# Attention into an expert layer on one Trainium2 core: weight conversion cut into single operations, scores and values on two shared banks, and a changed order of the fold

## The chip, the cores and the metric

The kernel runs on one core of a Trainium2 chip. The metric is the device time of one execution in microseconds (us). A core has TensorE (PE, with its weight loads as PEld), VectorE (DVE), ScalarE (ACT), GpSimd (POOL) and SyncE (SP), which here issues every transfer; TensorE writes to eight banks of PSUM memory, and VectorE and ScalarE empty them.

## The reference

Eight batches of 12 heads, 448 positions, 64 columns a head. The heads' scores are mixed with each other ahead of the softmax and behind it; the attention output is the input of an expert layer without a nonlinearity.

```python
scores = scale * np.matmul(q, k.transpose(0, 1, 3, 2))
scores = np.einsum('bhij,hg->bgij', scores, w_pre)
attn = np.exp(scores - np.max(scores, axis=-1, keepdims=True))
attn = attn / (np.sum(attn, axis=-1, keepdims=True) + 1e-09)
attn = np.einsum('bhij,hg->bgij', attn, w_post)
x = np.matmul(attn, v)                     # then (B*S, H*D) = (3584, 768)
a = x @ w1                                 # 768 x 1024
b = x @ w2
h = a * b @ w3                             # 1024 x 1024
out = h @ w_out                            # 1024 x 768
```

The expert weights come as 64-bit floats, and the kernel turns them into 32-bit floats itself.

## The kernel before

**The loop.** `run` walks through 360 steps, 45 a batch. A step handles 10 query rows of all 12 heads as one tile of 120 rows. In step n `softmax(n)` takes the row minimum (`mn`, VectorE L246, of negated scores) and the exponential (`e`, ScalarE L249); `scale(n-1)` makes the weights of the second mixing (`sa`, `ri`, `w`, VectorE); `split_r(n+2)` splits fetched scores into a high and a low part (`rh` on VectorE L226, `rl` on GpSimd L227); `post(n-2)` mixes the exponentials (`pso`, TensorE L272, bank 4), and ScalarE copies the result into `mt` (L278) at the end of the step; `mix(n+1)` mixes the next scores (`psm`, banks 2 and 3). Each engine runs its instructions strictly in the order in which the program issues them, and that order is written out here by hand: by this loop, by tables of steps, and by the lists `ends`, `soon` and `later`, which hold copies, second parts and stores back to the end of the step or to the next one.

**Scores.** Those of batch 0 (`qk_first`, `psz`, L158) come in 24 units, the last 18 of them in steps 0 to 14. Those of later batches come from `qk` (`psq`, L193 and L194, two matmuls a unit, 48 units a batch), ahead of `post` in their step, on banks 0 and 1 in turn; ScalarE copies them into `st` (L198), and they go to memory (`raw_d`) and come back as `r` four steps ahead of their use. `split_kq` makes the operands of a head: ScalarE writes `qh` (L181, 128 partitions, from queries that were loaded twice, `load_kq`) and half of `kk` (L182), GpSimd the low parts `ql` (L183) and the other half of `kk` (L184). Batch 1's units lie in steps 12 to 37, those of a later batch b in 45 steps from 45(b-1) - 6.

**Values.** In steps 17, 20, 32, 35, 47, 50 and so on (six a batch) `av` multiplies finished columns of `mt` with the values (`psa`, L303), in bank 5 up to the pair stage. Behind it ScalarE copies the result out (`xh` or `xd`), and in batch 0 VectorE takes the low part (`xl`).

**Conversion.** A piece of weights (128 x 384) is loaded as words (`cs`), ScalarE squares its upper words (`cm`, L102), VectorE makes four operations on it (`ca`, `ca`, `ca`, `cx`, L112 to L116, with bank 5 between them), ScalarE and GpSimd split the result into two parts (`two_parts`, L121 and L122: `fo`, `fw` or `wu`). A generator (`converting`) does a whole piece in a step, and none in a step with values, since those hold bank 5. 40 pieces belong to the fold, 32 to the two first weights.

**Fold and experts.** `folding` multiplies w3 with w_out into one matrix (`psf`, L361, 16 groups of 24 matmuls in banks 6, 7 and 1), in the background of steps 2 to 48; `share` says how many matmuls a step takes, and `there(p)` how many the pieces p made so far allow. From step 50 (`SWITCH`) the background are experts: batch 0 and 1 alone (`eg`, `eo`, L523 and L554, from step 53, `E_AT`, on) and, from step 187 (`PAIR`), three pairs of batches (`e`, L703) to the end. The first weights are converted from step 48 on while batch 0's experts use them (up to `LATE`, step 107).

## Time and profile before

| | us |
|---|---|
| median of 3 runs | 1639.13 (1638.95 to 1643.07) |
| the profiled execution | 1639.43 |
| its span in the profile | 1637.7 |
| TensorE busy | 1579.9 (96%) |
| VectorE busy | 1030.6 (63%) |
| ScalarE busy | 997.3 (61%) |
| GpSimd busy | 1068.5 (65%) |
| transfers | 446.10 MB, 272 GB/s on average |

Spans and busy times are those of the one profiled execution. A row of the profile names a line, an engine, an operation and its tiles as out<-in; the figures are busy time, the mean of one, and the idle time of the engine just ahead, with what ended it. Matmuls are pipelined, and their ends are modelled, so TensorE may be busy in the profile and still be below its pace: the distance of one step's `psm` to the next tells more.

### The profile page before, as it was taken

The page shows a single profiled execution, that of the slowest core. Times are in us where ns is not written, and L with a number is a line of the kernel's source. Part 1 is how long each engine was busy: PE and PEld are TensorE (multiplying, and loading weights), DVE is VectorE, ACT ScalarE, POOL GpSimd, SP SyncE. Part 2 cuts the span into 40 slices and gives each one's busy share as a digit, 9 for nine tenths or more (in the row PEclk, how much of TensorE's full clock was granted, in tenths as well). Part 3 has the DMA queues.
Part 4 walks back from the last instruction along what each step waited for, and adds up shares of the span by engine and source line. Part 5 has one row for each costly group of instructions (what it writes and reads, how often), then busy time and mean ns, then how long its engine had stood idle before and what let it go on. Part 6 is the DMA issues. An engine that isn't in the chain of part 4 may idle for free. (4 is left out here: it accounts for less than half of the span.)

```text
span 1637.7 us, 31687 instructions
## 1 busy us (share of the span) xinstructions
PE 1579.9 (96%) x10528; PEld 1414.0 (86%) x10528; DVE 1030.6 (63%) x2302; ACT 997.3 (61%) x2413; POOL 1068.5 (65%) x902
## 2 busy tenths in 40 slices
PE   5999999999999999999999999999999999999999
PEld 2578997887898888889899898899999898999988
DVE  5967768778747767863465565745555557634573
ACT  4877657677666776776666666666765554542321
POOL 1346546667657788885576776876675666655774
PEclk7999999999999999999999999999999999999999
DMA  8988879898899999999978977889978756678875
GB/s 263 342 269 275 255 223 302 277 310 288 264 279 310 321 341 315 323 335 306 312 240 279 290 243 238 257 270 309 305 248 250 238 188 196 211 229 302 281 233 179
DMA packets 233906, 446.10 MB, mean 272 GB/s; under 512 B 21838, under 2 KB 159054, under 8 KB 233678
## 3 DMA queue, kind: packets, MB, share of 16 engines
q1 hardware_dynamic: 233742, 444.08, 84.6%
q8 instruction: 83, 1.36, 0.4%
q14 instruction: 81, 0.66, 0.1%
HBM read 309.90 MB, written 134.09 MB: 271 GB/s over the span
## 5 line engine op out<-in xcount | busy, mean ns | idle before, releaser
L227 POOL TENSOR_TENSOR rl<-r,rh 120x448 fp32r<-120x448 f32 (+1 forms) x340 | 425.0, 1250 | 321.9 <-DVE rh L226 108.0
L246 DVE TENSOR_REDUCE mn<-psm 120x1 f32<-120x448 f32 x360 | 223.8, 622 | 410.1 <-PE psm L240 395.1
L249 ACT ACTIVATE e<-psm,mn 120x448 f32<-120x448 f32 x360 | 228.5, 635 | 348.1 <-DVE sa L258 293.4
L272 PEld LDWEIGHTS pso<-w,e 120*112 120x112 f32 (+1 forms) x2880 | 345.5, 177 | 49.4 <-ACT mt L278 35.0
L272 PE MATMUL pso<-w,e 120*112 120x120 f32 (+1 forms) x2880 | 358.9, 267 | 20.6 <-ACT mt L278 20.2
L703 PE MATMUL e<-eh,wu 128*128 128x448 f32 x1008 | 304.4, 371 | 1.1 <-DVE c L657 1.1
L278 ACT COPY mt<-pso 112x480 f32<-112x480 f32 x360 | 206.9, 575 | 14.9 <-PE pso L272 9.9
L703 PEld LDWEIGHTS e<-eh,wu 128*128 128x128 f32 x1008 | 187.3, 188 | 16.1 <-DVE c L657 1.9
L226 DVE CAST rh<-r 120x448 fp32r<-120x448 f32 (+1 forms) x340 | 189.9, 559 | 4.1 <-DMA r<-raw_d 3.0
L703 PE MATMUL e<-el,wu 128*128 128x448 f32 x504 | 187.6, 372 | 2.4 <-POOL el L642 2.4
L198 ACT COPY st<-psq 112x448 f32<-112x448 f32 x336 | 173.3, 527 | 25.8 <-DMA raw_d<-st 25.7
L303 PE MATMUL psa<-mt,v 112*64 112x150 f32 (+1 forms) x2304 | 156.9, 292 | 1.9 <-DMA v<-v 1.9
L183 POOL TENSOR_TENSOR ql<-kq,qh 128x448 fp32r<-128x448 f32 x84 | 99.2, 1181 | 85.1 <-ACT qh L181 84.9
L303 PEld LDWEIGHTS psa<-mt,v 112*64 112x64 f32 x2304 | 143.6, 137 | 8.1 <-DMA v<-v 2.3
L657 DVE TENSOR_TENSOR c<-c,e 128x448 f32<-128x448 f32 x168 | 101.2, 615 | 70.4 <-PE e L703 65.8
L193 PE MATMUL psq<-kk,qh 128*112 128x448 f32 x336 | 125.7, 374 | 8.0 <-ACT st L198 7.8
L238 PE MATMUL psm<-rh,wph 120*120 120x448 f32 (+1 forms) x340 | 129.6, 381 | 0.0
L523 PE MATMUL eg<-xh,wu 128*128 128x448 f32 x384 | 127.3, 381 | 0.0
L240 PE MATMUL psm<-rl,wph 120*120 120x448 f32 (+1 forms) x340 | 124.1, 365 | 0.6 <-POOL rl L227 0.5
L239 PE MATMUL psm<-rh,wpl 120*120 120x448 f32 (+1 forms) x340 | 124.2, 365 | 0.0
L194 PE MATMUL psq<-kk,ql 128*112 128x448 f32 x336 | 122.8, 365 | 0.0
L642 POOL TENSOR_TENSOR el<-x,eh 128x448 fp32r<-128x448 f32 x90 | 105.7, 1195 | 9.3 <-DMA x<-x_d 5.3
(114 smaller groups left out, 2961.7 us busy)
## 6 DMA issues: line engine op xcount, KB each, us to landing
r<-raw_d SPq DMA_DIRECT2D x352, 210.0 KB, 4.1
raw_d<-st SPq DMA_DIRECT2D x168, 392.0 KB, 4.7
wu<-w_d SPq DMA_DIRECT2D x104, 384.0 KB, 5.6
wu<-s_d SPq DMA_DIRECT2D x96, 384.0 KB, 4.4
v<-v SPq DMA_DIRECT2D x144, 224.0 KB, 5.1
kq<-kq SPq DMA_DIRECT2D x42, 672.0 KB, 7.0
wu<-w_d SPq DMA_DIRECT2D x51, 512.0 KB, 5.9
wu<-s_d SPq DMA_DIRECT2D x36, 512.0 KB, 4.4
```

The source lines that it names most:

```text
L193: nc.tensor.matmul(p, qh[:, cols], kk, start=True, stop=False)
L198: copy(st[:, c % 2], p)
L226: nc.vector.tensor_copy(rh[:K], r[:K])
L227: nc.gpsimd.tensor_tensor(rl[:K], r[:K], rh[:K].bitcast(F32), op=ALU.subtract)
L238: nc.tensor.matmul(p[:K, :S], self.wph[:K, :K], rh[:K], start=True, stop=False)
L246: nc.vector.tensor_reduce(mn[:K], p[:K, :S], axis=AX.X, op=ALU.min)
L249: nc.scalar.activation(e[:K], p[:K, :S], AF.Exp, bias=mn[:K], scale=-1.0, accum_out=sm[:K])
L272: nc.tensor.matmul(p[:, j, :, :w], e[:K, j * JT:(j + 1) * JT], w2[:K, :, :w], start=True, stop=True)
L278: self.ends.append((4, lambda: copy(dst, p[:, :, :, :w])))
L303: nc.tensor.matmul(self.psa[rows, g % 3, :W], v[:, j, rows], mt[:, j, 2 * g + s, :W], start=(j == 0), stop=(j == NJ - 1))
L523: nc.tensor.matmul(p, u[:, k % (K1 // 2), x], xs[y][:, k], start=(k == 0 and t == 0), stop=(k == K1 - 1 and t == 2))
L703: nc.tensor.matmul(p, w[:, k, x], ops[m, k][y], start=(k == 0 and t == 0), stop=(k == nk - 1 and t == 2))
```

## The change

- Conversion goes by single operations. `begin_conversion`, ahead of the softmax, splits the piece made before and squares the next; `convert` issues one VectorE operation. Up to step 48 a step makes four, none in step 0; afterwards two in even and three in odd steps, steps with values included, as far as `room` lets it run ahead of the matmuls.
- Values take one of the banks 0 and 1, in turn with the scores (`turn`), until the pair stage. Bank 5 is the conversion's alone.
- Batch 1's scores lie in steps 16 to 40, those of batch b in 45 steps from 45(b-1) - 4, none in a step with values. A step's first unit stays ahead of `post`; a second and third come behind it.
- The fold takes w3's columns and w_out's halves in another order: pieces come as w3's columns 0, w_out's first half, w3's columns 1, w_out's second half, then the other columns; the first four groups are (0, 0), (1, 0), (0, 1), (1, 1), so the second needs no more of w_out than the first. The even spread begins at step 16 (`FOLD`); ahead of it 24 matmuls may be done up to step 9 and 48 up to step 15, as far as the pieces made allow. `SWITCH` is 49, `E_AT` is 51.
- Queries are loaded once per pair of heads (2 instead of 3 planes, three buffers instead of two). ScalarE copies them into both halves of `qh`; `ql` has two fixed tiles, zeroed at the start in the half that isn't written.
- At the start the remaining queries of pair 0 are loaded ahead of `wpre`; step 0 has one unit of first scores instead of two.

Two places in the order. The first is TensorE in steps 11 and 12 (`psz` first scores, `psq` batch 1's scores, `psf` fold, `pso` second mixing). Before:

```order
L235 MATMUL psm11_742<-r11_549,wsc_138 120x448
L158 MATMUL psz2_3_0_769<-kqz2_126 112x448
L158 MATMUL psz2_3_1_770<-kqz2_126 112x448
L272 MATMUL pso9_782<-w29_712,e9_650 112x120 x4
L235 MATMUL psm12_787<-r12_593,wsc_138 120x448
L158 MATMUL psz3_3_0_817<-kqz3_127 112x448
L158 MATMUL psz3_3_1_818<-kqz3_127 112x448
L193 MATMUL psq1_0_0_824<-kk1_0_694,qh1_0_692 112x448
L194 MATMUL psq1_0_0_824<-kk1_0_694,ql1_0_693 112x448
L193 MATMUL psq1_0_1_829<-kk1_0_694,qh1_0_692 112x448
L194 MATMUL psq1_0_1_829<-kk1_0_694,ql1_0_693 112x448
L272 MATMUL pso10_839<-w210_765,e10_707 112x120 x4
```

In the changed kernel, the same engine and steps:

```order
L238 MATMUL psm11_724<-r11_536,wsc_143 120x448
L160 MATMUL psz2_3_0_750<-kqz2_130 112x448
L160 MATMUL psz2_3_1_751<-kqz2_130 112x448
L365 MATMUL psf0_1_765<-fo_147,fw1_677 128x384 x4
L275 MATMUL pso9_770<-w29_689,e9_635 112x120 x4
L365 MATMUL psf0_1_765<-fo_147,fw1_677 128x384 x5
L238 MATMUL psm12_780<-r12_580,wsc_143 120x448
L160 MATMUL psz3_3_0_802<-kqz3_131 112x448
L160 MATMUL psz3_3_1_803<-kqz3_131 112x448
L365 MATMUL psf0_1_765<-fo_147,fw1_677 128x384 x4
L275 MATMUL pso10_821<-w210_745,e10_684 112x120 x4
L365 MATMUL psf0_1_765<-fo_147,fw1_677 128x384 x5
```

Nine fold matmuls of the second group (w3's second columns, w_out's first half) stand in each of these steps, and the scores of batch 1 have left step 12.

The second place is step 90, where weights are converted for the experts. VectorE before (`rh` splits scores, `ca` and `cx` are the conversion):

```order
L246 TENSOR_REDUCE mn90_5312<-psm90_5304 120x1
L258 TENSOR_SCALAR sa89_5317<-sm89_5262 96x1
L259 RECIPROCAL ri89_5318<-sa89_5317 96x1
L262 TENSOR_SCALAR w289_5319<-wpo_140,ri89_5318 96x12x8
L226 CAST rh92_5323<-r92_5194 120x448
L112 TENSOR_SCALAR ca66_5338<-cs66_5226 128x384
L113 SCALAR_TENSOR_TENSOR ca66_5338<-cs66_5226,ca66_5338 128x384
L114 SCALAR_TENSOR_TENSOR ca66_5338<-cs66_5226,ca66_5338 128x384
L116 SCALAR_TENSOR_TENSOR cx66_5342<-cm66_5336,ca66_5338 128x384
L246 TENSOR_REDUCE mn91_5367<-psm91_5356 120x1
```

VectorE after the change:

```order
L249 TENSOR_REDUCE mn90_5311<-psm90_5294 120x1
L261 TENSOR_SCALAR sa89_5316<-sm89_5259 96x1
L262 RECIPROCAL ri89_5317<-sa89_5316 96x1
L265 TENSOR_SCALAR w289_5318<-wpo_145,ri89_5317 96x12x8
L229 CAST rh92_5322<-r92_5202 120x448
L138 SCALAR_TENSOR_TENSOR cx65_5330<-cm65_5254,ca65_5278 128x384
L131 TENSOR_SCALAR ca66_5334<-cs66_5181,ca66_5334 128x384
L249 TENSOR_REDUCE mn91_5364<-psm91_5351 120x1
```

Two conversion operations stand ahead of the next minimum instead of four. ScalarE in the same step before (`st` a score copy, `ea` an expert copy):

```order
L249 ACTIVATE e90_5314,sm90_5315<-psm90_5304,mn90_5312 120x448
L198 COPY st3_1_2_5277<-psq3_1_3_5327 112x448
L121 CAST wu25_5333<-cx65_5290 128x3x128
L102 ACTIVATE cm66_5336<-cs66_5226 128x384
L529 COPY ea0_5_5360<-eg0_5_0_5176 128x448
L278 COPY mt1_2_4644<-pso88_5348 112x48x10
L249 ACTIVATE e91_5369,sm91_5370<-psm91_5356,mn91_5367 120x448
```

ScalarE after:

```order
L252 ACTIVATE e90_5313,sm90_5314<-psm90_5294,mn90_5311 120x448
L201 COPY st3_1_0_5274<-psq3_1_1_5326 112x448
L201 COPY st3_1_2_5346<-psq3_1_2_5343 112x448
L281 COPY mt1_2_4640<-pso88_5338 112x48x10
L146 CAST wu25_5359<-cx65_5330 128x3x128
L116 ACTIVATE cm66_5362<-cs66_5181 128x384
L252 ACTIVATE e91_5366,sm91_5367<-psm91_5351,mn91_5364 120x448
```

The split `wu` and the square `cm` moved from ahead of `mt` to between `mt` and the next exponential.

The diff, cut to its core:

```diff
-    def converting(self, jobs):
...
-            if 0 <= n < len(jobs):
-                made = self.to_f32(s, m, f"{self.n_made}")
-                self.n_made += 1
-            yield
+    def ask_words(self):
+        if self.c_asked < len(self.c_jobs):
+            self.c_words.append(self.words(self.c_jobs[self.c_asked][0], f"{self.c_asked}"))
+            self.c_asked += 1
+
+    def begin_conversion(self):
+        if self.c_made is not None:
+            self.c_jobs[self.c_parts][1](self.c_made)
+            self.c_made = None
+            self.c_parts += 1
+        if self.c_square is None and self.c_words:
+            s = self.c_words[0]
+            m = self.cx.tile([128, CW], F32, tag="m", name=f"cm{self.c_piece}", bufs=1)[:, :s.shape[1]]
+            self.nc.scalar.activation(m, s[:, :, 1].bitcast(F32), AF.Square)
+            self.c_square = m
+
+    def convert(self):
...
+        if self.c_op == 0:
+            self.ask_words()
+            self.c_a = self.bank(5, f"ca{self.c_piece}").bitcast(I32)[:, :n]
+        a = self.c_a
+        if self.c_op == 0:
+            nc.vector.tensor_scalar(a, top, 3, 0x3FFFFFFF, op0=ALU.logical_shift_left, op1=ALU.bitwise_and)
+        elif self.c_op == 1:
...
+        else:
...
+            self.c_made, self.c_square = x, None
+            self.c_words.pop(0)
+            self.c_piece += 1
+        self.c_op = (self.c_op + 1) % 4
     def load_kq(self, b, p):
-        t = self.kp.tile([128, 3, S], F32, tag="kq", name=f"kq{b}_{p}")
+        t = self.kp.tile([128, 2, S], F32, tag="kq", name=f"kq{b}_{p}", bufs=3)
...
-        ql = self.kp.tile([128, S], F32R, tag="ql", name=f"ql{b}_{h}")
+        ql = self.low_q[s]
...
-        nc.scalar.copy(qh, t[:, s])
-        nc.scalar.copy(kk[a], t[a, 2])
-        q_lo.tensor_tensor(ql, t[:, s], qh.bitcast(F32), op=ALU.subtract)
-        k_lo.tensor_tensor(kk[z], t[a, 2], kk[a].bitcast(F32), op=ALU.subtract)
+        nc.scalar.copy(qh[a], t[a, 0])
+        nc.scalar.copy(kk[a], t[a, 1])
+        nc.scalar.copy(qh[z], t[a, 0])
+        q_lo.tensor_tensor(ql[a], t[a, 0], qh[a].bitcast(F32), op=ALU.subtract)
+        k_lo.tensor_tensor(kk[z], t[a, 1], kk[a].bitcast(F32), op=ALU.subtract)
...
-            self.i_psa = self.next_bank() if self.pairs else 5
+            self.i_psa = self.next_bank() if self.pairs else self.turn()
...
-        yield from columns[0]
         for q in range(2):
+            yield from columns[q]
             for k in range(KF):
...
-        for f in range(1, KF):
+        for f in range(2, KF):
             yield from columns[f]
...
+        order = [(0, 0), (1, 0), (0, 1), (1, 1)] + [(f, half) for f in range(2, KF) for half in range(2)]
+        for n, (f, half) in enumerate(order):
+            w = self.fw[f]
+            i = 6 + n % 2 if n else 1
...
+    def turn(self):
+        self.n_turn += 1
+        return self.n_turn % 2
...
+        self.low_q = [cp.tile([128, S], F32R, name=f"ql{s}") for s in range(2)]
+        for s in range(2):
+            nc.gpsimd.memset(self.low_q[s][(1 - s) * D:(2 - s) * D].bitcast(F32), 0.0)
...
+        nc.sync.dma_start(self.kq0s[0][:, JT + S:], self.kq0[0][:, JT + S:])
         w = self.kp.tile([128, S], F32R, tag="qh", name="wpre_s").bitcast(F32)[:GI, :GI]
...
-            firsts.setdefault((u - HP) * 15 // (HP * NJ - HP), []).append((u % HP, u // HP))
+            firsts.setdefault((u - HP - 1) * 14 // (HP * NJ - HP - 1) + 1, []).append((u % HP, u // HP))
...
-            first, per, ahead = (12, 26 / 48, 2) if b == 1 else ((b - 1) * NB - 6, 45 / 48, 3)
+            first, last, ahead = (16, 41, 2) if b == 1 else ((b - 1) * NB - 4, b * NB - 4, 3)
+            steps = [n for n in range(first, last) if n not in avs]
             for u in range(H * NJ):
                 h, c = divmod(u, NJ)
-                n = first + int(u * per)
+                n = steps[u * len(steps) // (H * NJ)]
...
+                    n = max(n - ahead, lasts[-2] + 1)
+                    splits.setdefault(n, []).append((b, h))
...
-        FOLD, SWITCH, E_AT = 18, NB + 5, NB + 8
+        FOLD, SWITCH, E_AT = 16, NB + 4, NB + 6
...
+            if n < 4:
+                self.softmax(n)
+            p = self.c_parts
+            if p < len(self.c_jobs):
+                self.begin_conversion()
+            if 4 <= n < N:
                 self.softmax(n)
...
+            qk(qks.get(n, [])[:1])
+            for _ in range(4 if 0 < n < SWITCH else n and 2 + n % 2):
+                i = self.c_piece
+                if not self.c_words or self.c_op == 3 and not self.c_square:
+                    break
+                if self.c_op == 0:
+                    if i < n_fold:
+                        f = (i - 2 * KF) // 3
+                        room = f < 2 or done >= (KF * 3 * 3 if f == 2 else 2 * KF * 3 * (f - 1))
                     else:
...
+                        room = i == n_fold and n == SWITCH - 1 or n >= SWITCH and 2 * done >= 3 * K1 * (i - n_fold - 4)
+                    if not room:
+                        break
+                self.convert()
...
             if n < SWITCH:
-                wanted += now
-                now = max(min(there(p), KF * 3 + wanted) - done, 0)
+                now = min(spread(n, SWITCH - 1, total), 18) if n >= FOLD else 0
+                now = min(there(p), max(done + now, KF * 3 * (1 if n < 10 else 2 if n < FOLD else 3))) - done
+            elif n < LATE:
+                now = min(3 * K1 // 2 * (p - n_fold) - done, spread(n, LATE, E_1))
...
             for x in avs.get(n, []):
                 self.av(*x)
+            qk(qks.get(n, [])[1:])
```

More of the change, by code (lines that the diff above doesn't have):

```diff
@@ L872, in run @@
             self.fetch(n)
-        next(fold_pieces)
-        next(fold_pieces)
+        piece()
         held()
-        next(fold_pieces)
-        next(fold_pieces)
+        piece()
         self.split_r(0)
@@ L911, in run @@
             if n == PAIR:
-                assert done >= 2 * E_1 + E_2 and unit_pieces is None and not self.jobs and not self.ys
+                assert done >= 2 * E_1 + E_2 and self.c_parts == len(self.c_jobs) and not self.jobs and not self.ys
                 self.do_ends()
```

178 lines of the change are left out of this document (71 added, 107 removed).

## The prediction

> **What bounds the kernel now.** I read the busy time by stretches first, with the cuts laid at step boundaries: steps 0 to 2 of the loop end at 38.7 us, step 9 at 64, step 19 at 112, step 47 at 243, step 56 at 276.4, step 104 at 451.7. Columns: length, then busy time (and instructions) of TensorE, its weight loads, VectorE, ScalarE and GpSimd, the granted clock, the share of the transfer engines, GB/s.
>
> ```profile
> 0.00:38.70 38.70, 21.89 (x58) 8.49 (x59) 19.30 (x42) 15.38 (x33) 4.92 (x9) 0.78 0.86 256
> 38.70:64.00 25.30, 25.12 (x125) 14.33 (x124) 22.76 (x51) 19.64 (x47) 6.02 (x6) 1.00 0.99 338
> 64.00:112.00 48.00, 42.81 (x230) 28.40 (x229) 36.14 (x88) 39.59 (x95) 23.91 (x22) 0.93 0.93 307
> 112.00:243.00 131.00, 128.15 (x907) 121.43 (x906) 93.37 (x230) 84.83 (x203) 75.62 (x69) 1.00 0.80 249
> 243.00:276.40 33.40, 29.34 (x206) 25.12 (x205) 26.57 (x70) 21.95 (x52) 18.89 (x17) 1.00 0.93 285
> 276.40:451.70 175.30, 165.78 (x1173) 147.50 (x1172) 140.06 (x359) 124.74 (x299) 120.58 (x108) 1.00 0.90 289
> 451.70:801.00 349.30, 340.83 (x2396) 309.99 (x2396) 222.06 (x464) 240.19 (x600) 255.20 (x200) 1.00 0.96 316
> 801.00:1637.70 836.70, 826.01 (x5446) 758.78 (x5444) 470.35 (x1002) 450.99 (x1092) 563.38 (x473) 1.00 0.79 251
> ```
>
> TensorE is busy for 1579.9 of the 1637.7 us (the rows' sum); the change takes no matmul away, so the 57.8 us of idle time and the time in which TensorE runs below its pace are all there is to win. The idle time is length less busy time: 16.8 us in the first row, then 0.2, 5.2, 2.9, 4.1, 9.5, 8.5, and 10.7 in the last row, which is half the program. The waits of TensorE say for whom (total, times, longest):
>
> ```profile
> PE pso L272 <- ACT mt L278: 20.2, 24, 2.0
> ...
> PE psq L193 <- ACT st L198: 7.8, 7, 2.2
> ```
>
> The largest is the value mixing `pso` waiting for ScalarE's copy `mt`, which empties its one bank.
>
> A busy TensorE is not one at its pace, so for the weight stage (276.4 to 451.7) I took steps that nothing disturbs. The first row is three plain steps in a row, the second a step with 24 value matmuls.
>
> ```profile
> 279.80:289.02 9.22, 9.22 (x59) 8.55 (x58) 8.61 (x25) 7.32 (x18) 7.39 (x8) 1.00 1.01 353
> 405.28:410.40 5.12, 5.12 (x62) 4.62 (x60) 2.15 (x6) 3.48 (x9) 4.69 (x4) 1.00 0.89 320
> ```
>
> A plain step needs 9.22 / 3 = 3.07 us, one with values 5.12. The stage has 42 and 6 of them: 159.7 us, and some 1.4 for seven steps with a fourth score matmul. It takes 175.3, so about 14 us are lost there. What one loss is made of, in order of time:
>
> ```profile
> 400.19 0.61 DVE L246 TENSOR_REDUCE mn<-psm 120x1 f32<-120x448 f32 x1
> ...
> 400.72 0.14 DVE L258 TENSOR_SCALAR sa<-sm 96x1 f32<-96x1 f32 x1
> 400.83 0.64 ACT L249 ACTIVATE e<-psm,mn 120x448 f32<-120x448 f32 x1 [2.12 <-DVE mn L246]
> 400.89 0.16 DVE L259 RECIPROCAL ri<-sa 96x1 f32<-96x1 f32 x1
> ...
> 401.09 0.27 DVE L262 TENSOR_SCALAR w<-wpo,ri 96x96 f32<-96x96 f32 x1
> ...
> 401.27 0.38 DVE L226 CAST rh<-r 120x448 fp32r<-120x448 f32 x1
> ...
> 401.58 0.55 DVE L112 TENSOR_SCALAR ca<-cs 128x384 int32<-128x384 int32 x1
> ...
> 401.87 0.52 ACT L121 CAST wu<-cx 128x384 fp32r<-128x384 f32 x1
> 402.16 0.56 DVE L113 SCALAR_TENSOR_TENSOR ca<-cs,ca 128x384 int32<-128x384 int32 x1
> 402.29 0.56 ACT L102 ACTIVATE cm<-cs 128x384 f32<-128x384 f32 x1
> ...
> 402.76 0.56 DVE L114 SCALAR_TENSOR_TENSOR ca<-cs,ca 128x384 int32<-128x384 int32 x1
> ...
> 403.15 0.58 ACT L278 COPY mt<-pso 112x480 f32<-112x480 f32 x1
> ...
> 403.45 0.55 DVE L116 SCALAR_TENSOR_TENSOR cx<-cm,ca 128x384 f32<-128x384 f32 x1
> ...
> 403.79 0.43 PE L272 MATMUL pso<-w,e 96*112 96x96 f32 x2 [1.70 <-ACT mt L278]
> ```
>
> VectorE's four conversion operations (`ca`, `ca`, `ca`, `cx`, a start-to-start of 0.6) follow the softmax work of the step (`mn` 0.61, `sa` 0.14, `ri` 0.16, `w` 0.27, `rh` 0.38: 1.56). A converting step thus asks 1.56 + 4 x 0.56 = 3.80 us of VectorE where TensorE needs 3.07, a step without asks 1.56. The next `mn` is late, then the exponential `e`, and on ScalarE the casts `wu` and `cm` (0.52, 0.56) stand ahead of `mt`; `pso` waits 1.70 us.
>
> **The change part by part.** I sum against this execution: 1637.7 us of span, 1639.43 with what lies around it, 0.3 above the median of the runs (1639.13).
>
> *Conversions by operations, weight stage.* Two operations in an even step, three in an odd one: VectorE is asked for 1.56 + 1.12 = 2.68 or 1.56 + 1.68 = 3.24 us, a mean of 2.96 against 3.07, and the value steps take their share, with 2.1 us more of room. `wu` and `cm` now stand after `mt` and ahead of the next `e`, where ScalarE waited for VectorE anyway (2.12 us in the row of `e` above). What replaces the wait is VectorE itself, with only 0.1 us to spare per plain step, and ScalarE in steps with a split. Of the 14 us I take 8 back; bounds 3 (only the order on ScalarE helps) and 13 (every step at its pace).
>
> *Steps 10 to 19, where transfers bind.* These ten steps take 48.0 us. With the orders of both kernels, TensorE's work in them is as good as equal: 16 score matmuls go later, 18 fold matmuls come in. Its losses there are 5.2 us idle and two stretches at half clock:
>
> ```profile
> PE psq L193 <- ACT st L198: 4.1, 2, 2.2
> PE psz L158 <- ACT sz L163: 1.1, 1, 1.1
> ```
>
> ```profile
> 71.30:74.80 3.50, 3.50 (x12) 1.86 (x12) 3.08 (x8) 2.81 (x7) 1.00 (x1) 0.51 1.04 357
> 91.80:95.30 3.50, 3.50 (x12) 2.61 (x12) 1.66 (x4) 3.48 (x9) 1.27 (x2) 0.51 1.01 336
> ```
>
> A stretch of 3.5 us at 0.51 costs 1.7, so 3.4 for both; with the idle time, 8.6. The clock fell after waits of 1.1 us and of 2.2 with 1.8. The Trainium skill ("TensorE: Matmul & The Clock Gate", in "Why this matters for your kernels") warns only of TensorE gaps above some 3 us; this trace has the clock halved after shorter ones, so I let the trace decide. By that rule the halved stretches would have another cause and stay, and the forecast would come out 3.4 us higher, 1623.8.
>
> Who makes TensorE wait there is ScalarE, whose copy `st` is in turn held by the stores that empty its buffers (first row below, 25.7 us over the span); the transfer engines are at 0.99 from 38.7 us on, moving 338 GB/s. The change moves four of the six score stores out of these steps and makes the three query loads a third smaller:
>
> ```profile
> L198 ACT COPY st<-psq 112x448 f32<-112x448 f32 x336 | 173.3, 527 | 25.8 <-DMA raw_d<-st 25.7
> ```
>
> ```profile
> raw_d<-st SPq DMA_DIRECT2D x168, 392.0 KB, 4.7
> ...
> kq<-kq SPq DMA_DIRECT2D x42, 672.0 KB, 7.0
> ```
>
> A query load falls from 672 to 448 KB (`t` has two planes instead of three). Saved: 4 x 0.40 + 3 x 0.23 = 2.3 MB; added: one piece of weights and one fold store, 0.39 MB each. Left are 1.5 MB, at 0.33 MB a us 4.5 us. Fewer waits of ScalarE bring the clock back as well; I take 5, with bounds 2 (only the loads count) and 8.6.
>
> *The start.* Step 0 had a conversion; now it has none, and its second unit of first scores goes to step 1.
>
> ```profile
> 22.04 0.62 DVE L246 TENSOR_REDUCE mn<-psm 120x1 f32<-120x448 f32 x1 [2.24 <-PE psm L235]
> ...
> 24.14 0.55 ACT L102 ACTIVATE cm<-cs 128x384 f32<-128x384 f32 x1 [3.91 <-DMA cs<-wo]
> ...
> 24.60 0.61 ACT L249 ACTIVATE e<-psm,mn 120x448 f32<-120x448 f32 x1
> ...
> 25.78 1.00 PE L158 MATMUL psz<-kqz 64*112 64x448 f32 x2 [1.31 <-ACT sz L163]
> ...
> 31.89 1.09 PE L158 MATMUL psz<-kqz 64*112 64x448 f32 x2 [3.54 <-DMA kqz<-kq]
> ```
>
> The exponential of step 0 waited behind `cm`, whose words landed at 24.1, and TensorE's second unit until 25.8 for a bank, with `psm` of step 1 behind it; at 31.89 a load ends a 3.5 us wait. Without `cm`, `e` can follow `mn`, done at 22.04 + 0.62 = 22.7, some 2 us sooner; the next weights are asked for one step later, which clears the queue for the loads of first scores. Against it, the remaining queries of pair 0 are put ahead of `wpre`, 0.17 MB, 0.5 us. I take 2.5, bounds 0 and 5.
>
> *Fold, steps 20 to 47.* TensorE idles 2.9 us now. Order by halves lets fold work begin at step 10; the pieces then run out, and steps 18, 19 and 23 have 2 or 3 fold matmuls where they had 13 or 14: those are VectorE's steps (four operations on top of its 1.56 us, 3.8 us or more). Fuller later steps give it back. Net 0.5, bounds -3 and 3.
>
> *The seam, 243 to 276.4.* Expert matmuls start at step 51 instead of 53, and the switch itself lies one step sooner; the first weights come at step 48 as they did. Of 4.1 us idle I take 2; bounds 0 and 4.
>
> *Queries loaded once, and the shared banks, everywhere.* A head's split now has three ScalarE copies of half the partitions instead of a whole and a half one:
>
> ```profile
> L181 ACT CAST qh<-kq 128x448 fp32r<-128x448 f32 x84 | 48.4, 576 | 1.5 <-PE psq L193 1.5
> L182 ACT CAST kk<-kq 64x448 fp32r<-64x448 f32 x84 | 47.5, 566 | 1.0
> ```
>
> Half the partitions cost as much as all (566 ns against 576), so each of 84 heads pays 0.57 us more: 48 us of ScalarE, 997 (the sum of its column) to 1045 of 1638. They are covered where ScalarE idles: it is busy 451 of 836.7 us in the last stretch and 240 of 349.3 before. GpSimd's operations keep their number, and I count their length as unchanged. Without that cover the 48 us would be on the path. The transfers shrink by 42 x 0.23 = 9.6 MB, which eases the stretch 451.7 to 801 (share 0.96). Scores no longer fall in value steps, so those lose a `psq` pair and plain steps sometimes hold two. After step 105 I count +1 in all; bounds -4 and 4.
>
> Sum: 8 + 5 + 2.5 + 0.5 + 2 + 1 = 19. 1639.4 - 19 = **1620.4 us**. The bounds of the terms, taken as independent, make 9 us either way: 1611 to 1630 for this case alone. A measurement of this kernel can tell some 0.3%, 5 us, from no change.
>
> **The rivals.**
>
> *The cover of one engine is the load of the next (half the gain).* VectorE with 0.1 us of room stays the pace-maker of the weight stage, and the stretch from 64 us on stays bound by transfers of weights that nobody moved. For it: VectorE's 140.1 of 175.3 us busy there, the same total after. Against: the losses sit in single steps after four operations in a row. Weight stage 3, early 2, start 2.5, seam 1, rest 0: 1639.4 - 8.5 = 1631. Chance 0.18.
>
> *ScalarE becomes the bound (slower).* The place is the steps with a split in the first 105 steps, 24 heads, and the same in later batches: `qh`, `kk`, `qh` again stand ahead of `e`, and `mt` behind that. ScalarE is already who ends 28 us of the waits above. If half of the 48 us shows, and the rest of the forecast holds, the time is 1620.4 + 24 = 1644. It decides from 19 / 84 = 0.23 us per head. Against: waits on `mt` after 801 us are 1.6 of 20.2. Chance 0.08.
>
> *Values and scores collide in two banks (no change).* There are 24 value steps before the pair stage; each now leaves values in bank 0 or 1, which the second score after it needs. In batch 0 VectorE's `xl` must read it first. At 0.75 us each, 18 us, the gain is gone: 1638. The longest wait of `psq` in the two-bank rotation was 2.2 us. The Trainium skill ("TensorE: Matmul & The Clock Gate", in "A second HAM failure mode: psum-queue depth-cycling") tells of a clock that oscillates when banks are cycled; from 112 us on the same rotation of scores ran at a clock of 1.00. Against: the score right after takes the other bank. Chance 0.07.
>
> *More is won:* the losses up to 451.7 us go, but for those ahead of the first softmax: 5 of the first row, 8.6, 2.9, 4.1 and 14, 35 us, or 1605. Chance 0.05.
>
> **How the numbers follow.** The forecast has 0.62. Faster by over 0.3%, below 1634.2: the forecast, the larger gain, and most of the half gain, 0.83. Within 0.3%: the banks and the rest of the half gain, 0.09. Slower by over 0.3%: 0.08. The range goes from 1608, where the larger gain begins, to 1636, above the half gain's middle by its own 5; outside are the slower case, the banks and half of the largest gain.
>
> **What would show it.** In the profile after: the stretch of steps 57 to 104 at about 167 us, with `pso` waits on `mt` under 5 us there; the clock at 1.00 from some 40 us on; step 20 near 104 us instead of 112.0; the step numbers can be counted by `psm`. ScalarE some 48 us busier with `qh` at 168 casts, and no new `psq` wait on `psa`'s readers. I am wrong if the weight stage stays near 175 us, if step 20 starts after 110, or if ScalarE's `mt` ends more than 20 us of waits.

## The result, and the profile after

The kernel after takes 1651.63 us (median of 4 runs, 1651.07 to 1653.65), the kernel before in the same series 1639.04. The ratio is 1.0075, with a 95% interval of 1.0055 to 1.0096: slower by 0.75%, where the forecast was 1620.4 us and the range ended at 1636. The profiled execution took 1652.15 us, its span is 1650.4.

The kernel after cut at the same steps as before (a step begins with its first `psm` matmul). Columns: length, busy time of TensorE with its instructions, the granted clock, the share of the transfer engines, GB/s.

```profile
0.00:38.80 38.80, 22.79 (x54) 0.74 0.83 254
38.80:64.00 25.20, 25.04 (x125) 1.00 0.95 308
64.00:110.80 46.80, 40.68 (x234) 0.96 0.88 274
110.80:252.60 141.80, 134.37 (x917) 0.98 0.75 234
252.60:288.90 36.30, 29.79 (x203) 0.91 0.84 257
288.90:461.20 172.30, 163.68 (x1162) 1.00 0.90 283
461.20:1650.40 1189.20, 1169.92 (x7843) 1.00 0.83 265
```

| steps | before, us | after, us | difference | forecast |
|---|---|---|---|---|
| start to 2 | 38.7 | 38.8 | +0.1 | -2.5 |
| 3 to 9 | 25.3 | 25.2 | -0.1 | 0 |
| 10 to 19 | 48.0 | 46.8 | -1.2 | -5 |
| 20 to 47 | 131.0 | 141.8 | +10.8 | -0.5 |
| 48 to 56 | 33.4 | 36.3 | +2.9 | -2 |
| 57 to 104 | 175.3 | 172.3 | -3.0 | -8 |
| 105 to the end | 1186.0 | 1189.2 | +3.2 | -1 |

Almost the whole loss lies in the fold stage, steps 20 to 47, and the gains forecast elsewhere came small or not at all. In the fold stage TensorE idles 141.8 - 134.4 = 7.4 us where it idled 2.9, and the clock is at 0.98 where it was at 1.00: two stretches of 3.4 us ran at half clock (from 140.6 and from 191.8 us), which cost some 1.7 us each (half their length). The waits of TensorE over the span:

```profile
PE pso L275 <- ACT mt L281: 26.6, 24, 5.4
PE psq L196 <- ACT st L201: 7.9, 10, 2.0
...
PE psq L196 <- DVE xl L328: 3.9, 6, 0.9
```

`mt` ends 26.6 us of waits where it ended 20.2, the longest 5.4 instead of 2.0; the third row is new. What such a wait looks like in the fold stage shows the timeline of steps 34 and 35 (from 187.7 us on; ScalarE, with TensorE and the stores of scores; L201 is the copy that was L198, L281 the copy `mt`):

```profile
182.98 0.34 SPq L205 DMA_DIRECT2D raw_d<-st  x1
...
184.90 0.53 ACT L201 COPY st<-psq 112x448 f32<-112x448 f32 x1
...
186.84 0.35 SPq L205 DMA_DIRECT2D raw_d<-st  x1
...
189.57 0.53 ACT L201 COPY st<-psq 112x448 f32<-112x448 f32 x1 [4.14 <-DMA raw_d<-st]
...
190.36 0.58 ACT L281 COPY mt<-pso 112x480 f32<-112x480 f32 x1
...
190.82 0.57 ACT L183 CAST qh<-kq 64x448 fp32r<-64x448 f32 x1
...
191.00 1.23 PE L275 MATMUL pso<-w,e 120*112 120x120 f32 x8 [2.35 <-ACT mt L281]
...
192.16 4.75 PE L306 MATMUL psa<-mt,v 112*64 112x150 f32 x48
```

`st` is a staging tile for two units of scores. There are two of them; the copy at 189.57 writes the tile whose store was issued at 182.98, and it stands 4.14 us until that store has landed. `mt` is behind it on ScalarE, `pso` waits 2.35 us for `mt`, and then the 48 value matmuls of step 35 take 4.75 us, where they took 3.28 before. The reason for that length is the clock (first row; columns as in the prediction's first fence, clock third from the end):

```profile
191.80:195.20 3.40, 3.40 (x27) 3.04 (x27) 0.00 (x0) 2.54 (x7) 3.25 (x4) 0.50 0.07 30
260.00:266.90 6.90, 3.81 (x24) 3.51 (x26) 4.16 (x10) 3.65 (x9) 3.21 (x3) 0.51 0.59 195
```

The clock is halved from 191.8 on for 3.4 us, after a gap of 2.35 us. The second row is the seam, steps 48 to 50:

```profile
255.94 0.38 SPq L373 DMA_DIRECT2D w_d<-fz  x1
...
260.58 0.51 ACT L146 CAST wu<-cx 128x384 fp32r<-128x384 f32 x1 [3.19 <-DMA w_d<-fz]
...
261.44 0.62 ACT L252 ACTIVATE e<-psm,mn 120x448 f32<-120x448 f32 x1
...
262.46 0.58 ACT L281 COPY mt<-pso 112x480 f32<-112x480 f32 x1
...
263.09 1.94 PE L275 MATMUL pso<-w,e 120*112 120x120 f32 x8 [5.43 <-ACT mt L281]
...
264.96 4.15 PE L306 MATMUL psa<-mt,v 112*64 112x148 f32 x48
```

The fold's memory is given to the weights there. The first weight cast `wu` waits 3.19 us for the last fold store to land, `e`, `st` and `mt` come behind it on ScalarE, `pso` waits 5.43 us, and the 48 value products of step 50 run at half clock, 4.15 us. The third new thing is the wait behind a step with values: VectorE's `xl` empties the bank that the second score of the next step takes.

```profile
106.06 0.52 ACT L201 COPY st<-psq 112x448 f32<-112x448 f32 x1
106.25 0.63 DVE L328 TENSOR_TENSOR xl<-psa,xh 128x450 fp32r<-128x450 f32 x1
...
107.02 0.43 PE L196 MATMUL psq<-kk,qh 128*112 128x448 f32 x1 [0.88 <-DVE xl L328]
```

(`xl` exists in batches 0 and 1, whose values stay on the chip, not in batch 0 alone as the sections above have it.)

### The profile page after: what moved, and what is told of

The parts are those of the page before. It is cut to its first block, busy times and chain, and to the rows that moved or that the text cites. A ratio compares the mean times of both kernels' runs of the same rounds, so it can differ in the third digit from the quotient of the medians.

```text
span 1650.4 us, 31788 instructions
## 1 busy us (share of the span) xinstructions
PE 1586.3 (96%) x10528; PEld 1418.1 (86%) x10528; DVE 1036.7 (63%) x2302; ACT 1046.5 (63%) x2497; POOL 1070.9 (65%) x904
## 5 line engine op out<-in xcount | busy, mean ns | idle before, releaser
L275 PE MATMUL pso<-w,e 120*112 120x120 f32 (+1 forms) x2880 | 359.3, 267 | 27.0 <-ACT mt L281 26.6
L281 ACT COPY mt<-pso 112x480 f32<-112x480 f32 x360 | 206.7, 574 | 11.3 <-PE pso L275 7.9
L201 ACT COPY st<-psq 112x448 f32<-112x448 f32 x336 | 173.5, 528 | 48.5 <-DMA raw_d<-st 28.9
L712 PEld LDWEIGHTS e<-eh,wu 128*128 128x128 f32 x1008 | 187.7, 188 | 15.1
L229 DVE CAST rh<-r 120x448 fp32r<-120x448 f32 (+1 forms) x340 | 187.7, 552 | 5.3 <-DMA r<-raw_d 4.6
L196 PE MATMUL psq<-kk,qh 128*112 128x448 f32 x336 | 132.1, 393 | 12.2 <-ACT st L201 7.9
L186 POOL TENSOR_TENSOR ql<-kq,qh 64x448 fp32r<-64x448 f32 x84 | 99.3, 1182 | 51.8 <-ACT qh L183 35.1
L527 PE MATMUL eg<-xh,wu 128*128 128x448 f32 x384 | 121.0, 374 | 0.0
```

The costliest lines, as they stand in the source:

```text
L196: nc.tensor.matmul(p, qh[:, cols], kk, start=True, stop=False)
L201: copy(st[:, c % 2], p)
L229: nc.vector.tensor_copy(rh[:K], r[:K])
L275: nc.tensor.matmul(p[:, j, :, :w], e[:K, j * JT:(j + 1) * JT], w2[:K, :, :w], start=True, stop=True)
L281: self.ends.append((4, lambda: copy(dst, p[:, :, :, :w])))
L712: nc.tensor.matmul(p, w[:, k, x], ops[m, k][y], start=(k == 0 and t == 0), stop=(k == nk - 1 and t == 2))
```

## The experiments

First theory: three places lose the time, each by a wait of its own: the staging tiles (the fold stage), the first weight cast (the seam), `xl` (behind value steps). First rival: ScalarE's third copy of each head, 48 us more work, is what bounds. All kernels were timed against the kernel before, in five series; before took 1637.86 to 1639.59 us in them, so kernels of different series are better compared by the ratio than by the median. The stages come from the profiled execution of each, and stages that no edit touches differ by up to 2 us between kernels (steps 120 to 149: 114.9 to 116.8 in all kernels made from after). The profiled execution was 7.4 us above the median for place, 3.8 for two, 2.9 for seam, 2.4 below it for best, and within 1.7 for the others; the stages of place and two are read with that in mind.

| kernel | median, us | ratio to before, interval | 10-19 | 20-47 | 48-56 | 57-104 |
|---|---|---|---|---|---|---|
| before | 1639.04 | 1 | 48.0 | 131.0 | 33.4 | 175.3 |
| after | 1651.63 | 1.0075 (1.0055 to 1.0096) | 46.8 | 141.8 | 36.3 | 172.3 |
| seam | 1649.26 | 1.0074 (1.0059 to 1.0089) | 48.3 | 142.3 | 34.7 | 172.4 |
| st3 | 1639.07 | 1.0007 (0.9996 to 1.0017) | 46.7 | 136.0 | 37.0 | 170.6 |
| planes | 1649.90 | 1.0071 (1.0056 to 1.0086) | 48.3 | 142.7 | 37.3 | 170.8 |
| place | 1655.86 | 1.0108 (1.0093 to 1.0123) | 56.3 | 142.8 | 37.1 | 170.8 |
| st3_xl | 1632.88 | 0.9960 (0.9947 to 0.9973) | 45.6 | 134.0 | 36.4 | 167.7 |
| st3_eat | 1639.63 | 1.0000 (0.9989 to 1.0011) | 46.7 | 136.0 | 37.5 | 169.5 |
| two | 1641.43 | 1.0013 (1.0002 to 1.0024) | 47.2 | 130.2 | 36.2 | 175.2 |
| before_st3 | 1639.98 | 1.0001 (0.9992 to 1.0010) | 49.5 | 132.0 | 33.8 | 176.6 |
| best | 1628.39 | 0.9944 (0.9929 to 0.9960) | 44.6 | 130.0 | 35.3 | 166.9 |
| best_sw | 1621.22 | 0.9896 (0.9880 to 0.9912) | 44.6 | 127.3 | 31.1 | 168.2 |
| best_cols | 1632.57 | 0.9965 (0.9952 to 0.9978) | 50.8 | 129.2 | 35.9 | 167.8 |
| best_sw3 | 1624.14 | 0.9913 (0.9899 to 0.9927) | 46.2 | 124.7 | 35.0 | 169.1 |
| whole | 1638.36 | 1.0002 (0.9992 to 1.0013) | 44.6 | 127.3 | 35.2 | 182.4 |
| sw_st2 | 1633.25 | 0.9964 (0.9949 to 0.9978) | 46.2 | 127.3 | 31.2 | 171.9 |
| after_sw | 1646.93 | 1.0052 (1.0035 to 1.0068) | 46.7 | 140.9 | 32.0 | 172.4 |

### First four: one suspect each

**seam.** The first weight cast comes a step later.

```diff
-            if p < len(self.c_jobs):
+            if p < len(self.c_jobs) and n != SWITCH:
                 self.begin_conversion()
```

> The kernel after, only that step 49 (the first after the fold) does not begin a conversion, so that the first weight cast, which waited 3.2 us on ScalarE for the last fold store, comes a step later. Theory (the seam's loss is that wait, the late mt and the half clock behind it: step 50 took 12.2 us for 4.7 us of matmuls): the wait of pso for mt of 5.4 us and the half clock at 260 go, 1646 us (1644 to 1648). Rival (something else in steps 48 to 57 holds it, and the next thing is as late): 1651 us, step 50 still over 9 us.

The wait of `pso` there fell from 5.4 to 2.8 us, but step 50 still took 10.7 us (12.2 before the edit), since the clock halved all the same, for 6.8 us, as long as in after (columns as in the table of steps above: length, busy time of TensorE, clock), and the time stayed: the rival, for the most part.

```profile
261.60:268.40 6.80, 5.94 (x42) 0.50 0.92 282
```

The weight cast lengthened the pause; it wasn't its only cause.

**st3.** Three staging tiles; the room comes from the query tiles, two instead of three.

```diff
-        t = self.kp.tile([128, 2, S], F32, tag="kq", name=f"kq{b}_{p}", bufs=3)
+        t = self.kp.tile([128, 2, S], F32, tag="kq", name=f"kq{b}_{p}", bufs=2)
...
-            self.st = self.kp.tile([JT, 2, S], F32, tag="st", name=f"st{b}_{h}_{c}")
+            self.st = self.kp.tile([JT, 2, S], F32, tag="st", name=f"st{b}_{h}_{c}", bufs=3)
```

> The kernel after with three staging tiles for the scores instead of two, and two query tiles instead of three to make the room. Theory (the fold stage loses because ScalarE's st copy waits for the store of the tile two before, 14.1 us in 8 waits between 85 and 240 us, up to 4.1 us, and mt and e stand behind it): those waits fall below 4 us, steps 20 to 48 go from 141.9 to about 134 us, the whole to 1643 us (1641 to 1647). Rival (ScalarE's third copy of each head is the cost and the waits only show slack): 1651 us, within 2.

12.6 us less than after (11 by the ratios), more than expected, and level with before. ScalarE's copy `st` had waited 28.9 us for its stores (the row of after); here no wait for them is left:

```profile
L201 ACT COPY st<-psq 112x448 f32<-112x448 f32 x336 | 173.5, 528 | 48.5 <-DMA raw_d<-st 28.9
```

```profile
110.00:246.00 136.00, 132.36 (x918) 0.99 0.79 245
```

The fold stage fell by 5.8 us, with TensorE idle 3.6 us in place of 7.4; most of the rest came in steps 150 to 239 (353.5 us against 357.6).

**planes.** Queries in three planes as before: `load_kq`, `split_kq` and the layout of `kq` are those of before.

```diff
-        nc.scalar.copy(qh[a], t[a, 0])
-        nc.scalar.copy(kk[a], t[a, 1])
-        nc.scalar.copy(qh[z], t[a, 0])
+        nc.scalar.copy(qh, t[:, s])
+        nc.scalar.copy(kk[a], t[a, 2])
```

> The kernel after with the queries in three planes as before: two ScalarE copies of a head instead of three, 84 x 0.57 = 48 us less on ScalarE. Theory (the copies lie in ScalarE's slack but for one or two places): 1650 us (1648 to 1652). Rival (ScalarE's third copy is what bounds, the case put at 1644 us in the prediction): 1640 us or less, the waits of pso for mt from 26.6 back to about 20 us.

1649.90, as the theory had it: taking away 48 us of ScalarE work, at the price of query loads of 672 KB in place of 448, brings nothing that the runs can tell. The rival falls.

**place.** Batch 1's scores in the steps of before, value steps included.

```diff
             steps = [n for n in range(first, last) if n not in avs]
+            if b == 1:
+                steps = [12 + int(u * 26 / 48) for u in range(H * NJ)]
```

> The kernel after with the second batch's scores placed as before (steps 12 to 37, one or two in a step, value steps too) and all else left. Theory (three scores in one step fill both staging tiles before the first store has landed): the waits of pso for mt in steps 20 to 48 (5.4 us) go and the stage takes about 135 us instead of 141.9, 1645 us (1642 to 1649). Rival (the order of the fold and its later start make the stage longer): 141 us for the stage, 1651 us.

Both times were wrong: 4 us slower (5 by the ratios), with a fold stage of 142.8 us, close to the rival's 141. Now scores stand in the value steps themselves, and there the collision of values and scores that the prediction named as a rival is at full size, 12.8 us in place of 3.9, the longest 3.1:

```profile
PE psq L196 <- DVE xl L328: 12.8, 9, 3.1
```

One wait of 3.1 and the clock, 0.88 in steps 10 to 19 where after has 0.96, lie ahead of step 20, and that stage takes 56.3 us (in an execution 7.4 us above the median). So the placement of after seems right in leaving out value steps; what is left to blame is that it puts three units in a step.

### Second four: the place, the bank, the seam again, and before

**two.** Batch 1's scores from step 13 on, so that 24 steps hold two each. Two staging tiles as in after.

```diff
-            first, last, ahead = (16, 41, 2) if b == 1 else ...
+            first, last, ahead = (13, 41, 2) if b == 1 else ...
```

> The kernel after with two staging tiles as it has, but the second batch's scores begin in step 13 instead of 16, so that 24 steps hold exactly two each and none holds three; still none in a value step. Theory (three scores in one step are what outruns two staging tiles and the ScalarE work of a head): ScalarE's waits for the stores between 85 and 240 us fall from 14.1 below 5 us and the time to about 1641 us (1637 to 1645). Rival (a store simply takes longer to land than two steps last, at any placement): the waits stay above 10 us and the time at 1650 us.

The fold stage falls by 11.6 us to 130.2, the clock there is back at 1.00, and the time falls to 1641.43. About 2 us of the 11.6 are five score units that now lie ahead of step 20; steps 10 to 47 together fall from 188.6 to 177.4, where before had 179.0. Putting the 48 units in 21 steps instead of 24, with three in six of them, was the cause there.

```profile
110.20:240.40 130.20, 128.09 (x908) 1.00 0.79 245
```

ScalarE's waits for the stores fell from 28.9 to 16.6 us over the span, and from 14.1 to none between 85 and 240 us; those left lie in later stages. Steps 57 to 104 took 175.2 us here, 2.9 more than in after, in an execution 3.8 us above the median; that isn't explained.

**st3_xl.** On st3: behind a value step, `xl` ahead of the row minimum.

```diff
             if n < 4:
                 self.softmax(n)
+            if avs.get(n - 1) and n < LATE:
+                self.do_soon()
```

> The kernel after with three staging tiles, and in the step behind a value step VectorE's xl comes ahead of the row minimum instead of behind five operations. Theory (the second score of that step waits for the bank that the values filled, 4.0 us in 6 waits, and about 1 us of step each in steps 66, 81 and 96): the waits of psq for xl fall below 1 us and the time by 3 to 5 us against the run with three staging tiles alone, 1635 us. Rival (mn and e come later by as much, so the wait only changes its name): within 1.5 us of that run, 1639 us.

Below before for the first time: 1632.88, 6.2 us under st3 (7.7 by the ratios), a little more than expected. The waits of `psq` for `xl` are gone from the list.

**st3_eat.** On st3: expert products from step 50 on.

```diff
-        FOLD, SWITCH, E_AT = 16, NB + 4, NB + 6
+        FOLD, SWITCH, E_AT = 16, NB + 4, NB + 5
```

> The kernel after with three staging tiles, and the first expert products begin in step 50 instead of 51. Theory (since the experiment that moved the weight cast only shortened the wait and the clock still halved through the 48 value products of step 50, the cause is that steps 48 to 50 hold 1.8 us of TensorE work each, less than the 3.3 us that a row block takes through VectorE and ScalarE): with nine products more in step 50 it takes at most 9 us in place of 13.0, the half clock goes or shortens, 1635 us (1633 to 1637). Rival (the wait comes ahead of those products, so they only stand behind it): step 50 plus 51 still 17 us, 1639 us.

The rival: step 50 took 13.5 us. Its pause comes ahead of the products that were added.

**before_st3.** The kernel before with `split_kq`, `load_kq` and the layout of after, and the tiles of st3.

```diff
-            self.st = self.kp.tile([JT, 2, S], F32, tag="st", name=f"st{b}_{h}_{c}")
+            self.st = self.kp.tile([JT, 2, S], F32, tag="st", name=f"st{b}_{h}_{c}", bufs=3)
```

> The kernel before with only two things changed: the queries loaded once (two query tiles, three ScalarE copies of a head) and three staging tiles. It says what the rest of the change is worth once the staging tile is no bound. Theory (the rest is worth something: fewer stalls in the weight stage): this kernel stays within 3 us of before, 1636 to 1641 us. Rival (before lost as much to the same stores, 18.2 us of ScalarE waits between 85 and 240 us, and the rest of the change is worth nothing or less): 1632 us or below.

No difference, 1.0001, as the theory had it; and since st3, with the same tiles, is at 1.0007, the rest of the change as it stood was worth nothing. But the 1.0001 is a sum: steps 150 to 239 take 5.0 us less than in before, and steps 10 to 149 take 4.6 more, two waits of `psq` for `ql` (4.1 us) among them. What the third tile alone is worth in before is therefore not shown. In the fold stage it brings nothing there (132.0 us against 131.0) and 5.8 us in after, although ScalarE waits for the same stores in steps 20 to 47 of both, first before, then after (in before_st3 these waits are gone):

```profile
ACT st L198 <- DMA raw_d<-st: 15.6, 9, 3.4
ACT st L201 <- DMA raw_d<-st: 14.1, 8, 4.1
```

The waits of TensorE for `mt` in these steps are none before and 3.8 us after. In before all units of a step stand ahead of `post`; after, the second and third behind it, and their copies come right ahead of `mt`. That this order is why the same wait costs more is an argument; no run moved it alone.

### Third four: the mends together, and the seam

**best.** st3, st3_xl and two in one kernel.

```diff
-            first, last, ahead = (16, 41, 2) if b == 1 else ...
+            first, last, ahead = (13, 41, 2) if b == 1 else ...
...
+            if avs.get(n - 1) and n < LATE:
+                self.do_soon()
```

> The kernel after with the three mends that took time out, together: three staging tiles, xl ahead of the row minimum behind a value step, and two scores in each of 24 steps from step 13 on. Theory (three scores in a step cost the fold stage, xl and the staging tiles the stages behind it, and they add): steps 20 to 48 take about 130 us as with two scores in a step, steps 57 to 105 about 167.7 as with xl first, the whole 1627 us (1624 to 1631). Rival (staging tiles and two scores in a step mend the same wait, and only one of them counts): 1633 us.

1628.39, in the expected range, with stages of 130.0 and 166.9 us as expected. But the mends add only in part: two units in a step brought 10.2 us alone and bring 4.5 on top of st3_xl (2.6 by the ratios), most of it in the fold stage (134.0 to 130.0). So the rival is half right: the third tile and two units a step mend partly the same waits.

**best_sw.** best, with the seam a step later.

```diff
-        FOLD, SWITCH, E_AT = 16, NB + 4, NB + 6
+        FOLD, SWITCH, E_AT = 16, NB + 5, NB + 7
```

> The same three mends, and the end of the fold one step later (the weights' memory changes hands at step 50 and the first expert products come at step 52, one later each; before: 50 and 53), so that one light step and not two stands ahead of the value step 50. Theory (two light steps in a row let TensorE run ahead of the softmax until it stops for 5 us and the clock halves through the value products): the wait of pso for mt of 5 us goes, steps 48 to 57 fall from 36 to about 31 us, 5 us below the run with the three mends alone. Rival (the wait only moves behind the value step): steps 48 to 57 within 1.5 us of 36, no difference.

7.2 us less, the fastest kernel here; between the profiled executions steps 48 to 56 are 4.2 us shorter and the fold stage 2.7, some of whose work moved into step 48. Steps 48 and 49, step 50, steps 51 to 56 in best:

```profile
237.20:241.80 4.60, 3.84 (x26) 1.00 0.85 250
241.80:253.60 11.80, 7.30 (x62) 0.71 0.80 259
253.60:272.50 18.90, 18.90 (x118) 1.00 0.89 260
```

and in best_sw:

```profile
234.70:240.80 6.10, 6.10 (x42) 1.00 0.72 242
240.80:247.20 6.40, 5.00 (x63) 1.00 0.97 304
247.20:265.80 18.60, 18.30 (x114) 1.00 0.93 287
```

Step 50 takes 6.4 us in place of 11.8, and the clock 0.71 is gone. In best steps 48 and 49 are light, with 3.84 us of matmuls together; in best_sw they have 6.10, and the stop is gone. That the light steps let TensorE use up its lead over the softmax is the reading that fits; the lead itself was not measured.

**best_sw3.** Two steps later.

```diff
+        FOLD, SWITCH, E_AT = 16, NB + 6, NB + 8
```

> The three mends, and the end of the fold two steps later (memory at step 51, first expert products at 53). Theory (filler ahead of the value step 50 keeps TensorE from running ahead): step 50 takes under 7 us; two light steps, 51 and 52, stand behind it and cost 3 to 4 us, so 2 to 4 us below the run with three mends alone. Rival (the light steps cost the same wherever they stand, since the softmax of a block takes its 3.3 us): no difference, within 1.5 us.

As expected, or a little better: step 50 takes 4.7 us, step 52 takes 5.8 where best_sw has 3.6, and the sum is 4.3 us under best. The gain shows in the fold stage (130.0 to 124.7), whose matmuls spread over two more steps, while steps 48 to 56 stay at 35.0.

**best_cols.** best, with the fold's order of before (columns of w3, all of w_out ahead of the second). The edit is cut to its core; the order of the pieces and the counts that go with it are those of before too.

```diff
-        order = [(0, 0), (1, 0), (0, 1), (1, 1)] + [(f, half) for f in range(2, KF) for half in range(2)]
+        order = [(f, half) for f in range(KF) for half in range(2)]
```

> The three mends, and the fold by whole columns of w_out first, as before, in place of halves. The prediction gave the steps 10 to 19 a gain of 5 us, of which the fold by halves (work that is there earlier) was a part; measured were 1.3 us. Theory (the halves bring filler into steps 10 to 16 but the stalls there are the first reads and scores, so little hangs on them): within 2 us of the run with the three mends, steps 10 to 20 within 2 us too. Rival (the halves are worth their 3 to 5 us and something else took the rest): 3 us or more longer.

The theory fell: 4.2 us longer, and 6.2 in steps 10 to 19, where the clock is 0.93 and best has 1.00. The halves are worth about as much as the prediction gave this stage, but the prediction gave it for fewer transfers and counted the halves as next to nothing (0.5 us, in the fold stage).

### Last three: the weight stage, the tiles, the seam alone

**whole.** best_sw, but from step 49 on a piece's four operations in one step, none in value steps.

```diff
-            for _ in range(4 if 0 < n < SWITCH else n and 2 + n % 2):
+            for _ in range(4 if 0 < n < SWITCH or n and not avs.get(n) else 0):
```

> The fastest kernel so far (the three mends and the seam one step later), but in the weight stage a piece's four VectorE operations stand in one step again and none in a value step, as before; the fold stage keeps its spread. Theory (the prediction's first term, 8 us in steps 57 to 104, is right in mechanism and the collisions hid it): the stage goes from 168.2 to about 174 us and the whole up by 5 us, 1626 us. Rival (the stage's gain is from elsewhere, so the term was wrong in cause too): the stage within 1.5 us of 168.2, 1621 us.

17.1 us longer; between the profiled executions 14.2 us lie in steps 57 to 104 and 4.1 in steps 48 to 56, which the edit changes too. So four operations in one step do cost time there: the mechanism of the prediction's first term, and more than its size. The stage is 7.1 us longer than in before, where four operations stood in a step as well; why they cost more in this order is not shown. TensorE's waits in that stage of whole, and then of best_sw:

```profile
PE pso L275 <- ACT mt L281: 8.5, 11, 1.9
PE psq L196 <- ACT st L201: 5.7, 5, 2.0
```

```profile
PE psq L196 <- ACT st L201: 2.6, 4, 0.9
PE pso L275 <- ACT mt L281: 2.2, 3, 1.1
```

**sw_st2.** best_sw with two staging and three query tiles, as in after.

```diff
-            self.st = self.kp.tile([JT, 2, S], F32, tag="st", name=f"st{b}_{h}_{c}", bufs=3)
+            self.st = self.kp.tile([JT, 2, S], F32, tag="st", name=f"st{b}_{h}_{c}")
```

> The fastest kernel so far with two staging tiles and three query tiles again. Theory (once no step holds three scores two tiles do nearly as well, and only the weight stage, where some steps hold two scores and the query loads stand beside them, loses): 1624 us (1621 to 1628). Rival (the stores need the third tile at any placement): 1631 us or more.

1633.25, 12 us more (11 by the ratios): the rival. With two units in a step the fold stage no longer needs the third tile (127.3 in both), but the stages behind do: steps 57 to 104 take 3.7 us more, 150 to 186 4.1, 187 to 239 3.8.

**after_sw.** after, with the two numbers of best_sw alone.

```diff
-        FOLD, SWITCH, E_AT = 16, NB + 4, NB + 6
+        FOLD, SWITCH, E_AT = 16, NB + 5, NB + 7
```

> The kernel after with the seam alone one step later. Theory (the seam's pause and half clock are a loss of their own, whatever the other three do): steps 48 to 57 from 36.2 to about 31 us, 1646 us (1644 to 1648). Rival (it helps only where the fold stage leaves time): 1651 us.

4.7 us less (3.8 by the ratios), and steps 48 to 56 fall from 36.3 to 32.0: a loss of its own.

The stages of the fastest kernel, best_sw (columns as at the top):

```profile
0.00:37.60 37.60, 21.60 (x55) 0.77 0.86 262
37.60:62.80 25.20, 25.03 (x126) 1.00 0.99 320
62.80:107.40 44.60, 41.49 (x243) 1.00 0.99 304
107.40:234.70 127.30, 125.37 (x894) 1.00 0.81 250
234.70:265.80 31.10, 29.40 (x212) 1.00 0.90 281
265.80:434.00 168.20, 163.13 (x1167) 1.00 0.92 295
434.00:1618.30 1184.30, 1168.35 (x7843) 1.00 0.84 266
```

## Why the prediction was wrong

**Fold, steps 20 to 47 (forecast -0.5, bounds 3 either way; measured +10.8).** This is the step that failed. It weighed only fold matmuls that move. "The change moves four of the six score stores out of these steps" counted the stores as gone, and did not follow them: 48 units that lay in 26 steps went into 21, six of which hold three. The prediction had the row that says who is sensitive to that (`st` idle 25.8 us for `raw_d<-st`), and used it for steps 10 to 19 alone. What the runs showed in its place: ScalarE's copies wait for the stores of their tiles, `mt` comes late behind them, TensorE stops for up to 2.35 us and restarts at half clock. Shown by two (130.2 us with two units a step) and st3 (136.0 with a third tile). Why waits of that size cost nothing in before is argued only, as said at before_st3.

**The seam (forecast -2, measured +2.9).** That the switch lies a step sooner was taken as a gain. It puts two light steps ahead of a value step. Shown by best_sw and after_sw, which fill the first of the two; the weight cast, the first theory, only lengthened the pause.

**Weight stage (forecast -8, measured -3.0).** Mechanism right, the size hidden: with `xl` first and a third tile it takes 166.9 to 168.2 us, and the forecast said 167; undone alone it costs 14.2. The waits for `mt` there were halved (first before, then after), to under the 5 us that the prediction named as its sign:

```profile
PE pso L272 <- ACT mt L278: 8.4, 10, 1.7
PE pso L275 <- ACT mt L281: 4.3, 7, 1.4
```

What took the gain back is the third rival's collision (167.7 us in st3_xl against 170.6 in st3) and the stores (3.7 us in sw_st2).

**Steps 10 to 19 (forecast -5, measured -1.2).** The transfers fell as forecast and a little more (307 GB/s over 48.0 us are 14.7 MB, 274 over 46.8 are 12.8), but the time did not follow, so transfers alone did not set it. TensorE idles 6.1 us there where it idled 5.2, with one halved stretch where it had two. `xl` and the three scores of step 16 are a part: st3_xl has 45.6 us, best 44.6, 3.4 under before, and without the fold by halves it is 50.8 (best_cols).

**The start (forecast -2.5, measured +0.1)** was mis-sized: step 3 begins at 38.8 us where it began at 38.7, since the load that ended a TensorE wait at 31.89 us ends one at 32.4 now, whatever is done before.

**After step 105 (forecast -1, measured +3.2).** The loss lies in steps 105 to 149, 168.5 us before and 172.2 after, where TensorE waits longer for `mt` (first before, then after):

```profile
PE pso L272 <- ACT mt L278: 1.6, 4, 0.5
PE pso L275 <- ACT mt L281: 6.2, 7, 1.5
```

None of the mends touches it: best has 170.9 us and 5.6 us of these waits. The queries loaded once are not the reason, for planes has 171.6 us and before_st3 169.0; which other part of the change is, stays open. Steps 150 to 239 take the same before and after (357.9 and 357.6 us); that a third tile saves some 4 to 8 us there (st3, sw_st2) is a gain that before and after both leave out.

**The rivals.** *ScalarE becomes the bound* gave 1644 and so the right side, for a wrong reason: planes shows that the copies cost nothing that the runs can tell. *The cover of one engine* gave 1631 and a weight stage 3 us shorter, which is what was measured, but by luck: with more VectorE work, not less (149.9 us busy in best_sw, 143.9 in after), the stage went down to 168.2 us, so VectorE was not what held it. *Values and scores collide* had a chance of 0.07 at 0.75 us for each of 24 steps; there were six waits of 0.65 on average, all in batches 0 and 1, which alone have `xl`, but mending them brought 6.2 us, more than the 3.9 of the waits. Its counter-argument, "the score right after takes the other bank", forgot the second score of that step. Its page of the Trainium skill ("TensorE: Matmul & The Clock Gate", "A second HAM failure mode: psum-queue depth-cycling") has no part in it as far as the rows show: where the two banks turn without such a wait (best_sw from 107.4 us on) the clock is 1.00.

**The clock.** The same page of the Trainium skill ("Why this matters for your kernels") warns only of gaps above some 3 us. Here too the trace disagrees: the row at 191.8 us shows 0.50 for 3.4 us after a gap of 2.35. The prediction was right to go by the trace, but drew the benefit only, not that new gaps can cost halved stretches: from 64 us on after has three of 3.4 us and one of 6.9, where before had two of 3.4. Not every such gap does: before had one of 2.0 us between 243 and 276.4 us, and the clock there is 1.00.

**The signs.** Of the prediction's three signs of being wrong two came: step 20 starts at 110.8 us, and `mt` ends 26.6 us of waits. The weight stage, at 172.3 us, lies between its 167 and its 175. ScalarE is 49 us busier (1046.5 where it was 997.3), as it said.

**Near the number by another way.** best_sw comes to 1621.22 us, next to the forecast of 1620.4. That is in part luck: it is another kernel, with changes that the prediction didn't have, and its fold stage is 3.7 us under before where 0.5 was forecast, its start 1.1 where 2.5 was.

## What to carry to other kernels

When a change takes work out of one stretch, follow it to where it lands and count there what it needs per step: buffers that are free only when a store has landed, and the place of its copies on an in-order engine. A gain on the bound engine can be real in full and still not be seen, when two or three small waits of other kinds come with it; take them out one at a time, and then together, before undoing the change. Lightening steps is no gain by itself: two light ones ahead of a heavy one made TensorE stop and restart at half clock.

## What was not expected of the hardware

Half clock came after gaps of 2.35 us (for 3.4 us) and 5.43 us (for 6.9 us); in the second case it fell during the gap and held 3.8 us beyond its end, so a pause of 5 us ahead of the 48 value products of step 50 made the step 12.2 us long in place of 6.4 in best_sw. A gap of 2.81 us, in the run seam, was followed by as long a stretch (6.8 us). A staging tile could be written again only 6.6 us after its store was issued (182.98 to 189.57), against a median of 4.9 from issue to landing over the span.
